# Thirty-two bytes under the feed-forward weights, and later, paced scatters and gathers, in a fused attention and expert kernel

## The chip, the core and the metric

The kernel runs on one core of one Trainium2 chip. The metric is the time of one execution on the device in microseconds (us), the median of several runs. A second, profiled execution left the trace from which all rows below are taken; it has a time of its own.

A core has a matrix engine (TensorE, PE in the rows; its weight loads are PEld), VectorE (DVE), ScalarE (ACT), GpSimd (POOL) and SyncE (SP), each with its own queue of instructions in order. Here SP starts the plain transfers, POOL the indirect ones (gathers and scatters by a table of row numbers), ACT eight loads of weights.

## The reference, cut to what matters

```python
scores = (1 / S) * np.matmul(z, z.transpose(0, 2, 1))        # 8 batches, S = 3072, z is 64 wide
x = u * np.matmul(np.maximum(scores, 0.0) ** 2, v)           # u, v: 8 x 3072 x 256
x = x.reshape(24576, 256)
e = argmax(x @ w_gate); g = softmax weight of e * sigmoid(x @ w_output_gate)[e]
x = g * (np.maximum(x @ w1[e], 0.0) @ w2[e])                 # 8 experts, 256 -> 1024 -> 256
h = x @ w_in; out = (h * sigmoid(h)) @ w_out                 # 256 -> 2048 -> 256
```

Attention without a softmax, then one expert out of eight for each token, then a feed-forward layer for all tokens.

## The kernel before, in words

Every large product is made of three matmuls of rounded 32-bit halves: a value is split into `hi` and `lo` (function `split`, line 104: a copy on ACT or DVE, then a subtraction on DVE), and hi x lo, lo x hi and hi x hi are added up. The matrix engine does them in three stages, one after the other.

**Attention** (line 641). 48 chunks q of 512 rows (six to a batch), each with 24 steps j; 1152 steps k in all. A step is eight matmuls of 512 columns: two for the scores of step k+3 (`s_step`, lines 269 and 270) and six for the values of step k (`v_step`, lines 297 to 299). Between the two stand ACT (`act_r`, line 275; `act_a`, line 280) and DVE (`dve_hl`: `hi` in line 108, `lo` in line 109). The rest is written into tables by step number with `at(k, ...)` and runs behind `dve_hl` of that step: loads of the next batch on SP (`z_load`, `v_load`, `u_load`), splits of its z and v (`z_prep1`, `v_prep`), copies of z's halves over to the other partitions (`z_prep2`, two transfers on SP, lines 198 and 199), and for each finished chunk `x_mul`, `x_hi`, `x_lo`, the transposes `x_tr` into the tile `z` (line 318), and the gate. When a chunk's row numbers are known, 16 scatters on POOL (`x_scatter`, line 466) write its tile `z` into the table `x_d` in device memory. For the first two chunks they are put at step 54 + 16 q + c, for the others spread over 24 steps from step 15 of the next chunk on. `z` has two buffers, so `x_tr` of chunk q waits for the scatters of chunk q-2.

`x_d` has to be zero where no token comes. SP writes the zeros, 26 transfers of up to 1 MB (`zero_pages`, line 165), at steps 5, 9 and 13 and then one in every second step up to 61. The framework orders a scatter and a zero transfer against each other as they stand in the program, since their rows can't be told apart.

`paced(i)` (line 113) lets an indirect transfer wait for the last DVE subtraction in the list `beat`; `dve_hl` and, in the last stage, `h2` append to it. Before the change, the scatters of all chunks but the last, and the gathers of the last stage from block 2 on, are paced.

**Experts** (line 939). 103 pages of 256 tokens, each with one expert, four steps each; 24 matmuls of 256 columns in a step (lines 742 and 763). The weights of a page come by gathers on POOL (line 684), are split on ACT and DVE (`w_split`), and results go out by scatters on POOL (line 770). The scatters of attention that are left over, and the last chunk's (at steps 39 to 54), are issued here. In the last 32 steps the tokens of the feed-forward's block 0 are gathered (line 811) and split.

**Feed-forward** (line 990). 48 blocks m of 512 tokens, 16 steps fc each. A step is twelve matmuls of 512 columns: six for `s2` of step k+3 (line 855) and six for `v2` of step k (lines 877 to 879). Between them ACT takes the sigmoid (line 862) and DVE does three operations (lines 863, 108 and 109, in `h2`). Each block's tokens come by 16 gathers on POOL (`y_gather`, line 811) and are scaled, transposed and split (`y_scale`, `y_tr`, `y_split`). Block 1's 16 gathers stand together between the expert stage and this loop, with no pacing; block 2's are put at fc = 6 to 15 of block 0. The product of line 855 reads `sc` tiles of PSUM of which there are two, so `s2` of step k+3 waits until DVE has read that of step k+1.

**Where tiles lie.** The build gives every tile a byte address in the partition. By their remainder when divided by 128: all operands of attention's large matmuls (`hi`, `lo`, `vh`, `vl`, `hh`, `ll`, `st`) lie at 32; all of the expert stage's (`x1h`, `x1l`, `w0b`, `h1`, `l1`, `w1b`) at 64; in the feed-forward the stationary weights `wi` and `wo` lie at 96, the moving values `yh`, `yl`, `h2`, `l2` at 64, but block 0's `yh0` and `yl0` at 96. The gate's matmuls (line 325) have weights at 32 and moving values at 96. Slices of these tiles begin at multiples of 512 bytes from their start. `wi`, `wo`, `yg0`, `yh0` and `yl0` are in the pool `wr`, which is at the right end of the partition and grows to the left.

Of the kernel before, what the change touches and what calls it, by code (L numbers as in the profile page):

```python
# [8 lines left out]
F32 = mybir.dt.float32  # L9
F32R = mybir.dt.float32r  # L10
# [20 lines left out]
P = 128  # L31
Q = 32
CH = 512
NCH = S // CH
NQ = B * NCH
NJ = S // P
NSTEP = NQ * NJ
NB = CH // Q
# [4 lines left out]
HD = D // 4  # L43
# [5 lines left out]
QL = NQ - 1  # L49
# [3 lines left out]
def fused_kernel(ctx: ExitStack, tc: tile.TileContext, uT, v, zT, wg, w1, w2, w_in, w_out, out):  # L53
# [43 lines left out]
    xp = xs.enter_context(tc.tile_pool(name="xp", bufs=1, side="right", reuse_waits="tile"))  # L97
    att = ExitStack()
    small = att.enter_context(tc.tile_pool(name="small", bufs=1))
    zp = att.enter_context(tc.tile_pool(name="zp", bufs=1))  # L100
# [3 lines left out]
    def split(hi, lo, src, eng="v"):  # L104
        if eng == "a":
            sc.activation(hi, src, AF.Copy)  # L106
        else:
            ve.tensor_copy(hi, src)  # L108
        return ve.tensor_sub(lo, src, hi.bitcast(F32))  # L109

    beat = []

    def paced(i):

        tc.add_manual_dep(
            i.ins, beat[-1].ins.name,
            mybir.DependencyInfo(mybir.DependencyClass.Sync, mybir.DependencyReason.DATA),
            reason="one indirect transfer at a time",
        )
# [64 lines left out]
        ZZ[b, c] = zz  # L184

    def z_prep1(b, c):
        hh = zp.tile([P, CH], F32R, name="hh", tag="hh", bufs=7)
        ll = zp.tile([P, CH], F32R, name="ll", tag="ll", bufs=7)
        split(hh, ll, ZZ.pop((b, c)), "v" if b == 0 and c < 2 else "a")
        HH[b, c], LL[b, c] = hh, ll  # L190

# [110 lines left out]
    XH, XL, Z, G = {}, {}, {}, {}  # L302

    def x_mul(q, dc):
        if dc == 0:
            XH[q] = xp.tile([P, 2, CH], F32R, name="xh", tag="xh", bufs=1)
            XL[q] = xp.tile([P, 2, CH], F32R, name="xl", tag="xl", bufs=1)
            Z[q] = xp.tile([P, NB, HD], F32, name="z", tag="z", bufs=2)
        ve.tensor_mul(UT[q][:, dc, :], ACC[q][dc], UT[q][:, dc, :])

    def x_hi(q, dc):
# [150 lines left out]
    def x_scatter(q, cs=range(NB)):  # L462

        before = XS.setdefault(q, [])
        for c in cs:
            i = gp_.indirect_dma_start(  # L466
                x_u, bass.IndirectOffsetOnAxis(ap=xi4[:, q * NB + c:q * NB + c + 1], axis=0),
                Z[q][:, c, :], None, bounds_check=NSLOT * 4 * T - 1, oob_is_err=False,
            )
            for o in before:  # L470
                tc.declare_no_dep(i.ins, o.ins, reason="scatters to different rows")
            if q < QL:
                paced(i)
            before.append(i)

    def gate_s(q):
# [86 lines left out]
    def at(k, f, *a, pe=False):  # L563
        (pe_tasks if pe else tasks).setdefault(k, []).append((f, a))

    for b in range(1, B):
        first = (b - 1) * NCH * NJ
        last = first + (NCH - 1) * NJ
        for c in range(NCH):
            at(first + c * NJ + 12, z_load, b, c)  # L570
            at(first + c * NJ + 20, z_prep1, b, c)
            at(first + c * NJ + 22 if c < 3 else last + 4 * (c - 3) + 4 if c < NCH - 1 else last + 22,
               z_prep2, b, c)
            s1_ = first + (c + 1) * NJ + 16 if c < 3 else last + (6, 15, 17)[c - 3]
            at(s1_ - 6, v_load, b, c)
            at(s1_, v_prep, b, c, 0)
            at(s1_ + 1, v_prep, b, c, 1)
# [10 lines left out]
    SSTEPS = [15 + (3 * c + 1) // 2 for c in range(NB)]  # L588
    ON_PE = (gate_mm, rank_mm, rep_mm, order1_mm, order2_mm)
    left = []  # L590
    for q in range(NQ - 1):
        for s, f, *a in XTASKS:
            at((q + 1) * NJ + s, f, q, *a, pe=f in ON_PE)
        for c in range(NB):
            k = 54 + q * NB + c if q < 2 else (q + 1) * NJ + SSTEPS[c]
            if k < NSTEP:
                at(k, x_scatter, q, [c])
            else:
                left.append((q, [c]))
# [3 lines left out]
    for job, q in zip(range(2 * NWJ), [q for q in range(1, NQ) if q % NCH < NCH - 1]):  # L603
        k = q * NJ
# [85 lines left out]
    def w_split(k, which):  # L690
        if k >= NS1:
            return
        t, fp = divmod(k, NSUB)
        if which == 0:
            src = raw1[t % 2][:, :, fp * 2 * P:(fp + 1) * 2 * P]
        else:
            src = raw2[t % 2][:, 2 * fp:2 * fp + 2, :]
        w = fp_.tile([P, 2, 2, 2 * P], F32R, name=f"w{which}b", tag=f"w{which}b", bufs=4)
        split(w[:, 0], w[:, 1], src, "a")
        WB[which, k] = w  # L700

    def x_gather(t):
# [30 lines left out]
    def s1(k):  # L733
        t, fp = divmod(k, NSUB)
        ps = ps_s.tile([P, 2, T], F32, name="s1", tag="sc")
        wb = WB.pop((0, k))
        for i in range(2):
            fs = slice(i * P, (i + 1) * P)
            n = 0
            for dc in range(2):  # L740
                for hl, xx in ((1, X1H[t]), (0, X1L[t]), (0, X1H[t])):
                    pe.matmul(ps[:, i, :], wb[:, hl, dc, fs], xx[:, dc, :], start=(n == 0), stop=(n == 5))  # L742
                    n += 1
        hi = mp.tile([P, 2, T], F32R, name="h1", tag="h1", bufs=4)
        lo = mp.tile([P, 2, T], F32R, name="l1", tag="l1", bufs=4)
        sc.activation(hi, ps, AF.Relu)
        ve.scalar_tensor_tensor(lo, ps, 0.0, hi.bitcast(F32), ALU.max, ALU.subtract)  # L747
        H1[k], L1[k] = hi, lo
# [26 lines left out]
    def w_load(dst, o, i):  # L775
        n = 4 * DFF // 4
        sc.dma_start(
            dst.rearrange("p a b c -> p (a b c)")[:, i * n:(i + 1) * n].bitcast(F32),
            wio_d[:, o + i * n:o + (i + 1) * n],
        )  # L780
# [23 lines left out]
    def y_gather(m, cs=range(NB)):  # L804
        if m >= NQ:
            return
        if m > 0 and m not in YG:
            YG[m] = lp.tile([P, NB, HD], F32, name="yg", tag="yg", bufs=3)
        n = (NFIRST if m == 0 else NSLOT) * 4 * T
        for c in cs:  # L810
            i = gp_.indirect_dma_start(  # L811
                YG[m][:, c, :], None, y_u[:n, :],
                bass.IndirectOffsetOnAxis(ap=yi4[:, m * NB + c:m * NB + c + 1], axis=0),
                bounds_check=n - 1, oob_is_err=False,
            )
            if m > 1:
                paced(i)

    def y_scale(m, h):
# [119 lines left out]
    for k in range(NS1):  # L939
        t, fp = divmod(k, NSUB)  # L940
        if k + L1K < NS1:
            s1(k + L1K)
        else:
            s2(k + L1K - NS1)
        for f, a in late.get(k, []):
            if f in ON_PE:
                f(*a)
        v1(k)
        if fp == 0:
            x1_prep(t + 1)  # L950
            if t + 3 >= 4:
                x_gather(t + 3)
        if fp == NSUB - 1 and t < NSLOT - 1:
            y_store(t)
        w_ahead(k)
        if k == NS1 - 24:
            sc.activation(npg, efl, AF.Sigmoid)
        if k in ahead:
            f, *a = ahead[k]
            f(*a)  # L960
        for f, a in late.get(k, []):
            if f not in ON_PE:
                f(*a)
        if k == 120:
            yops = y_index()
        if k > 120 and yops:
            yops.pop(0)()
        if k == 72:
            xs.close()
            wr = moe.enter_context(tc.tile_pool(name="wr", bufs=1, side="right", reuse_waits="tile"))  # L970
            wi = wr.tile([P, 2, 2, DFF], F32R, name="wi")
            wo = wr.tile([P, 2, FC2, D], F32R, name="wo")
            ylast = wr.tile([P, 2, D], F32, name="ylast")
            YG[0] = wr.tile([P, NB, HD], F32, name="yg0")
            YH[0] = wr.tile([P, 2, CH], F32R, name="yh0")
            YL[0] = wr.tile([P, 2, CH], F32R, name="yl0")
        if k in range(80, 160, 10):
            w_load(*((wi, 0), (wo, 4 * DFF))[k >= 120], k // 10 % 4)
    assert not yops
# [3 lines left out]
    for k in range(L1K):  # L983
        h2(k)
    y_store(NSLOT - 1)
    y_gather(1)
    for k in range(L1K, LOOK):
        s2(k)
        h2(k)
    for k in range(NS2):  # L990
        m, fc = divmod(k, FC2)
        if k + LOOK < NS2:
            s2(k + LOOK)
            h2(k + LOOK)
        if fc == 1 and m > 0:
            o_store(m - 1)

        if m > 0:
            y_gather(m + 2, [c for c in range(NB) if fc == 1 + 7 * c // 8])
        elif fc >= 6:  # L1000
            y_gather(2, [c for c in range(NB) if fc == 6 + 9 * c // 15])
        for f, when in ((y_scale, (8, 9) if m == 0 else (3, 4)), (y_tr, (9, 10) if m == 0 else (6, 8)),
                        (y_split, (10, 11) if m == 0 else (7, 9))):
            if fc in when:
                f(m + 1, when.index(fc))
        v2(k)
# [36 lines left out]
```

## Time and profile before

| | |
|---|---|
| Median of the runs | 5558.6 us (5557.41 to 5558.87, 3 runs) |
| Profiled execution: its own time | 5563.38 us |
| its span, first to last instruction | 5561.7 us |
| TensorE busy in the span | 99% |
| DVE, ACT and POOL busy | 80%, 51%, 37% |
| Mean granted clock of TensorE | 0.998 |

The own time of the profiled execution is 1.7 us over its span, and 4.8 us over the median. In the rows, PE's matmuls overlap (the next one starts before the modelled end of the one before), so what a matmul costs is the distance from start to start, not its duration. An idle time in brackets at the end of a row is that before the instruction, with what ended it.

### The profile page before, as it was taken

How to read it: one execution, taken by the hardware profiler on the slowest of the kernel's cores; microseconds unless marked ns; L12 is line 12 of the kernel's file. 1: busy time of each engine (PE TensorE's matmuls, PEld its weight loads, DVE VectorE, ACT ScalarE, POOL GpSimd, SP SyncE). 2: the span in 40 equal slices, each digit the busy share in tenths (PEclk: the TensorE clock that was granted, in tenths of full speed). 3: DMA queues.
4: the chain of work that ended last, by engine and by line, in shares of the span. 5: the costliest groups of instructions: out<-in, count | busy, mean ns of one | idle time of the engine just before them, and what ended most of it. 6: DMA issues, size and time to landing. Idle time of an engine off the chain costs nothing. (4 is left out here: it accounts for less than half of the span.)

```text
span 5561.7 us, 84596 instructions
## 1 busy us (share of the span) xinstructions
PE 5516.5 (99%) x28952; PEld 4694.6 (84%) x28952; DVE 4469.0 (80%) x9832; ACT 2861.0 (51%) x5076; POOL 2055.8 (37%) x1961
## 2 busy tenths in 40 slices
PE   9999999999999999999999999999999999999999
PEld 7788888888888887999999998888888888888887
DVE  8899999999999887878777776777777777777776
ACT  7676777777777766666666664222222222222222
POOL 0433333333333334443333344333333333333331
PEclk9999999999999999999999999999999999999999
DMA  7212121211122101254222221000000000000000
GB/s 259 79 53 60 52 60 53 65 56 56 58 58 58 43 24 54 79 176 140 84 78 76 86 67 35 24 24 24 24 24 24 27 24 24 24 24 24 24 24 20
DMA packets 160243, 314.99 MB, mean 57 GB/s; under 512 B 58560, under 2 KB 66752, under 8 KB 152384
## 3 DMA queue, kind: packets, MB, share of 16 engines
q0 software_dynamic: 95152, 156.97, 9.7%
q1 hardware_dynamic: 63504, 144.22, 8.1%
q10 hardware_dynamic: 1152, 8.39, 0.4%
q8 instruction: 226, 3.70, 0.3%
q14 instruction: 209, 1.71, 0.1%
HBM read 346.83 MB, written 112.72 MB: 83 GB/s over the span
## 5 line engine op out<-in xcount | busy, mean ns | idle before, releaser
L466 POOL DMA_INDIRECT x_d<-z,xi x768 | 794.0, 1034 | 1447.2 <-DVE lo L109 788.5
L811 POOL DMA_INDIRECT yg<-y_d,yi x768 | 807.0, 1051 | 1284.1 <-DVE l L109 1169.5
L862 ACT ACTIVATE sg<-s 128x512 f32<-128x512 f32 x768 | 458.8, 598 | 1599.1 <-PE s L855 1484.0
L855 PE MATMUL s<-yh,wi 128*128 128x512 f32 x3072 | 1089.8, 396 | 5.1 <-DVE sg L863 4.1
L275 ACT ACTIVATE r<-sc 128x512 f32<-128x512 f32 x1152 | 688.8, 598 | 547.3 <-PE sc L270 486.1
L863 DVE TENSOR_TENSOR sg<-s,sg 128x512 f32<-128x512 f32 x768 | 530.7, 691 | 486.6 <-ACT sg L862 480.0
L297 PE MATMUL acc<-hi,vl 128*128 128x512 f32 x2304 | 908.1, 394 | 3.1 <-DVE hi L108 3.1
L298 PE MATMUL acc<-lo,vh 128*128 128x512 f32 x2304 | 900.6, 391 | 1.6 <-DVE lo L109 1.6
L299 PE MATMUL acc<-hi,vh 128*128 128x512 f32 x2304 | 898.3, 390 | 0.0
L109 DVE TENSOR_TENSOR lo<-a,hi 128x512 fp32r<-128x512 f32 x1152 | 798.1, 693 | 39.5
L280 ACT ACTIVATE a<-r 128x512 f32<-128x512 f32 x1152 | 726.2, 630 | 98.8 <-DVE lo L109 73.0
L855 PEld LDWEIGHTS s<-yh,wi 128*128 128x128 f32 x3072 | 577.2, 188 | 145.5 <-DVE sg L863 4.5
L742 PE MATMUL s<-x1h,w0b 128*128 128x256 f32 x3296 | 662.9, 284 | 11.3 <-DVE w0b L109 9.9
L763 PE MATMUL acc<-w1b,h 128*128 128x256 f32 x3296 | 660.7, 283 | 0.0
L877 PE MATMUL acc<-h,wo 128*128 128x512 f32 x1536 | 608.0, 396 | 0.0
L878 PE MATMUL acc<-l,wo 128*128 128x512 f32 x1536 | 608.0, 396 | 0.0
L879 PE MATMUL acc<-h,wo 128*128 128x512 f32 x1536 | 608.0, 396 | 0.0
L855 PE MATMUL s<-yl,wi 128*128 128x512 f32 x1536 | 607.5, 396 | 0.0
L108 DVE CAST hi<-a 128x512 fp32r<-128x512 f32 x1152 | 490.7, 426 | 93.3 <-ACT a L280 83.0
L742 PEld LDWEIGHTS s<-x1h,w0b 128*128 128x128 f32 x3296 | 544.9, 192 | 12.8 <-DVE w0b L109 9.6
L109 DVE TENSOR_TENSOR l<-sg,h 128x512 fp32r<-128x512 f32 x768 | 532.2, 693 | 26.5
L763 PEld LDWEIGHTS acc<-w1b,h 128*128 128x128 f32 x3296 | 543.7, 192 | 0.1
(200 smaller groups left out, 9647.6 us busy)
## 6 DMA issues: line engine op xcount, KB each, us to landing
x_d<-zero SPq DMA_DIRECT2D x25, 1024.0 KB
vr<-in_v_dram SPq DMA_DIRECT2D x48, 512.0 KB
ut<-in_uT_dram SPq DMA_DIRECT2D x48, 512.0 KB
out_dram<-ot SPq DMA_DIRECT2D x48, 512.0 KB
zz<-in_zT_dram SPq DMA_DIRECT2D x96, 128.0 KB
x_d<-z,xi POOLq DMA_INDIRECT x768
yg<-y_d,yi POOLq DMA_INDIRECT x768
st<-hh SPq DMA_DIRECT2D x47, 128.0 KB
```

Source lines behind the costliest of these rows:

```text
L109: return ve.tensor_sub(lo, src, hi.bitcast(F32))
L275: sc.activation(r, SC.pop(k), AF.Relu, scale=1.0 / S)
L280: sc.activation(a, RR.pop(k), AF.Square)
L297: pe.matmul(ACC[q][dc], vl[:, j % 4, ds_], hi, start=(j == 0), stop=False)
L298: pe.matmul(ACC[q][dc], vh[:, j % 4, ds_], lo, start=False, stop=False)
L299: pe.matmul(ACC[q][dc], vh[:, j % 4, ds_], hi, start=False, stop=(j == NJ - 1))
L466: i = gp_.indirect_dma_start(x_u, bass.IndirectOffsetOnAxis(ap=xi4[:, q * NB + c:q * NB + c + 1], axis=0), Z[q][:, c, :], None, bounds_che ...
L742: pe.matmul(ps[:, i, :], wb[:, hl, dc, fs], xx[:, dc, :], start=(n == 0), stop=(n == 5))
L763: pe.matmul(acc[:, h, :], x[:, i, ts], wb[:, hl, i, :], start=first, stop=end, skip_group_check=True)
L811: i = gp_.indirect_dma_start(YG[m][:, c, :], None, y_u[:n, :], bass.IndirectOffsetOnAxis(ap=yi4[:, m * NB + c:m * NB + c + 1], axis=0), bo ...
L855: pe.matmul(ps, wi[:, hl, dc, fs], xx[:, dc, :], start=(n == 0), stop=(n == 5))
L877: pe.matmul(acc, wo[:, 1, fc, es], hi, start=(fc == 0), stop=False)
```

## The change

Five things are done:

- The pool `wr` gets one more tile of 32 bytes at its end. Since the pool's right end stays, `wi`, `wo`, `ylast`, `yg0`, `yh0` and `yl0` begin 32 bytes earlier: at a remainder of 64 by 128 instead of 96. No other tile of the feed-forward moves.
- The scatters of chunk q are issued no earlier than step 76 + 6 (16 q + c) / 5. This moves those of chunks 0 to 7 (chunk 0: steps 54 to 69 before, 76 to 94 after); from chunk 8 on the steps are those of before. `z` gets a third buffer.
- To pay for it, `hh` and `ll` get six buffers in place of seven, and the split of the next batch's z goes from step 20 to 26 after the start of a chunk (step 2 of the chunk that follows), its copies on SP from 22 to 28 where they stood there. Tiles of attention move by 4096 bytes or not at all.
- `w_split` of the expert stage also appends to `beat`, and the last chunk's scatters are paced too. The scatters left over from chunk 46 (ten of them), which waited for a subtraction long done, wait for the newest weight split.
- Block 1's 16 gathers go from the front of the feed-forward loop into block 0's steps fc = 0 to 7, two in a step and paced; block 2's go to fc = 8 to 15, two in a step.

```diff
@@ z_prep1
-        hh = zp.tile([P, CH], F32R, name="hh", tag="hh", bufs=7)
-        ll = zp.tile([P, CH], F32R, name="ll", tag="ll", bufs=7)
+        hh = zp.tile([P, CH], F32R, name="hh", tag="hh", bufs=6)
+        ll = zp.tile([P, CH], F32R, name="ll", tag="ll", bufs=6)
@@ x_mul
-            Z[q] = xp.tile([P, NB, HD], F32, name="z", tag="z", bufs=2)
+            Z[q] = xp.tile([P, NB, HD], F32, name="z", tag="z", bufs=3)
@@ x_scatter
-            if q < QL:
-                paced(i)
+            paced(i)
@@ for b in range(1, B): for c in range(NCH):
-            at(first + c * NJ + 20, z_prep1, b, c)
-            at(first + c * NJ + 22 if c < 3 else last + 4 * (c - 3) + 4 if c < NCH - 1 else last + 22,
+            at(first + c * NJ + 26, z_prep1, b, c)
+            at(first + c * NJ + 28 if c < 3 else last + 4 * (c - 3) + 4 if c < NCH - 1 else last + 28,
                z_prep2, b, c)
@@ for q in range(NQ - 1): for c in range(NB):
-            k = 54 + q * NB + c if q < 2 else (q + 1) * NJ + SSTEPS[c]
+            k = max((q + 1) * NJ + SSTEPS[c], 76 + 6 * (q * NB + c) // 5)
@@ w_split
-        split(w[:, 0], w[:, 1], src, "a")
+        beat.append(split(w[:, 0], w[:, 1], src, "a"))
@@ y_gather
-            if m > 1:
+            if m > 0:
                 paced(i)
@@ pool wr
             YL[0] = wr.tile([P, 2, CH], F32R, name="yl0")
+
+            wr.tile([P, 8], F32, name="wr_gap")
@@ ahead of the feed-forward loop
     y_store(NSLOT - 1)
-    y_gather(1)
@@ in the feed-forward loop
         if m > 0:
             y_gather(m + 2, [c for c in range(NB) if fc == 1 + 7 * c // 8])
-        elif fc >= 6:
-            y_gather(2, [c for c in range(NB) if fc == 6 + 9 * c // 15])
+        elif fc < 8:
+            y_gather(1, [2 * fc, 2 * fc + 1])
+        else:
+            y_gather(2, [2 * fc - 16, 2 * fc - 15])
```

## Rows read from the trace of the kernel before

**Rows 1.** The page's first part: busy time, share and instructions of each engine.

```profile
PE 5516.5 (99%) x28952; PEld 4694.6 (84%) x28952; DVE 4469.0 (80%) x9832; ACT 2861.0 (51%) x5076; POOL 2055.8 (37%) x1961
```

**Rows 2.** Windows: length, busy us (count) of PE, PEld, DVE, ACT, POOL; PEclk; DMA.

```profile
104.00:150.00 46.00, 45.61 (x208) 36.89 (x207) 40.55 (x119) 30.86 (x55) 9.09 (x8) 1.00 0.53 183
150.00:210.00 60.00, 49.51 (x206) 39.17 (x205) 44.46 (x128) 31.95 (x58) 30.02 (x30) 0.89 0.22 67
210.00:255.00 45.00, 45.00 (x207) 36.88 (x206) 41.47 (x121) 31.11 (x55) 16.22 (x17) 1.00 0.14 42
500.00:2100.00 1600.00, 1598.74 (x7279) 1307.11 (x7279) 1464.85 (x4231) 1123.26 (x1966) 584.77 (x569) 1.00 0.18 53
...
2400.00:3300.00 900.00, 899.86 (x7499) 899.62 (x7497) 688.21 (x1114) 589.99 (x1094) 340.04 (x312) 1.00 0.32 105
3405.00:3440.00 35.00, 29.90 (x121) 23.49 (x120) 20.15 (x34) 5.82 (x11) 22.07 (x22) 0.95 0.11 24
...
3500.00:5500.00 2000.00, 2000.00 (x8573) 1610.11 (x8572) 1457.34 (x2414) 518.25 (x894) 738.07 (x704) 1.00 0.09 24
```

**Rows 3.** Timeline of PE, attention: start us, duration us, instruction.

```profile
561.92 0.39 PE L269 MATMUL sc<-hh,st 128*128 128x512 f32 x1
...
570.99 0.39 PE L269 MATMUL sc<-hh,st 128*128 128x512 f32 x1
```

**Rows 4.** Timeline of PE, two score products of the feed-forward's block 0.

```profile
3402.00 0.39 PE L855 MATMUL s<-yh,wi 128*128 128x512 f32 x1
...
3404.73 0.40 PE L877 MATMUL acc<-h,wo 128*128 128x512 f32 x1
```

**Rows 5.** Waits between 140 and 195 us: who for whom, us, times, longest.

```profile
ACT r L275 <- remote: 8.7, 1, 8.7
...
PE sc L269 <- ACT r L275: 7.6, 2, 7.2
POOL x_d L466 <- DMA x_d<-zero: 7.3, 1, 7.3
...
DVE z L318 <- DMA x_d<-z,xi: 6.2, 1, 6.2
```

**Rows 6.** Waits of SP's queue over the whole span.

```profile
SPq L165 <- DMA x_d<-z,xi: 37.0, 4, 13.4
```

**Rows 7.** Timeline of POOL, first scatter, and a run of scatters.

```profile
116.36 1.17 POOL L466 DMA_INDIRECT x_d<-z,xi  x1 [113.20 <-DVE lo L109]
...
154.01 1.40 POOL L466 DMA_INDIRECT x_d<-z,xi  x1 [5.54 <-DVE hi L108]
...
182.32 0.97 POOL L466 DMA_INDIRECT x_d<-z,xi  x1 [0.30 <-issue]
```

**Rows 8.** Timeline of ACT at the start of the feed-forward.

```profile
3425.45 0.60 ACT L862 ACTIVATE sg<-s 128x512 f32<-128x512 f32 x1 [5.11 <-PE s L855]
3432.57 1.09 ACT L862 ACTIVATE sg<-s 128x512 f32<-128x512 f32 x2 [6.52 <-remote]
```

**Rows 9.** Timeline of POOL there: the ends of two runs of gathers.

```profile
3406.65 1.05 POOL L811 DMA_INDIRECT yg<-y_d,yi  x1 [2.53 <-DVE l L109]
...
3429.65 0.99 POOL L811 DMA_INDIRECT yg<-y_d,yi  x1 [0.30 <-issue]
3435.42 1.00 POOL L811 DMA_INDIRECT yg<-y_d,yi  x1 [4.78 <-DVE l L109]
...
3453.99 1.00 POOL L811 DMA_INDIRECT yg<-y_d,yi  x1 [0.51 <-issue]
```

**Rows 10.** Timeline of DVE at the change from attention to experts.

```profile
2199.56 0.71 DVE L724 STREAM_TRANSPOSE xt<-xg 128x512 f32<-128x512 f32 x1 [9.35 <-DMA xg<-x_d,xidx]
```

**Rows 11.** The tile `ll`: its instruction, count, ns min/median/max, first and last start.

```profile
L109 DVE TENSOR_TENSOR ll<-zz,hh x48: 682/686/727, 5.9 to 1919.4; 128x512 fp32r<-128x512 f32 x48
```

**Rows 12.** Line 325, the gate's matmuls: the same columns.

```profile
L325 PE MATMUL lg<-xl,gm x96: 394/396/403, 68.4 to 2253.4; 128*128 128x512 f32 x96
```

**Rows 13.** Timeline of DVE in a batch's last chunk, around step 8.

```profile
539.11 0.69 DVE L109 TENSOR_TENSOR vl<-vr,vh 128x512 fp32r<-128x512 f32 x1 [1.48 <-ACT vh L106]
```

## The prediction, made before the changed kernel was run

> **What bounds the kernel now.** I read the busy shares first. TensorE is busy 99% of the span, the next engine 80% [rows 1], so the time is what its matmuls cost from start to start, plus its few gaps. The windows of the three stages come next [rows 2]. They give three costs. In attention, 40 matmuls of 512 columns lie between the two rows of [rows 3]: 570.99 - 561.92 = 9.07 us, 226.75 ns each. In the expert stage 7499 matmuls of 256 columns fill 900 us: 120.0 ns each. In the feed-forward 8573 matmuls of 512 columns fill 2000 us: 233.3 ns each. At the granted clock of 1.00 (the level of 2.4 GHz) 512 columns are 213.3 ns and 256 are 106.7 ns. So attention and experts both pay 13.3 ns on each matmul, and the feed-forward pays 20.0 ns on each. The reader is to see that the same kind of matmul is 6.6 ns dearer in the last stage, with no engine behind: DVE is busy 73% there, POOL 37%.
>
> The windows also show where TensorE stood still. From 104 to 150 us it did 208 matmuls and from 150 to 210 us 206; from 3405 to 3440 us it did 121. The waits and the queues then say why [rows 5 to 9].
>
> **The change, part by part.**
>
> *The 32 bytes.* In attention and in the expert stage stationary and moving tiles have the same remainder by 128; in the feed-forward they are 32 apart. The trace holds one trial of this: block 0's `yh0` and `yl0` lie as `wi` does. Two score products of that block that run without other matmuls between them, twelve matmuls of line 855, take 3404.73 - 3402.00 = 2.73 us [rows 4], 227.5 ns each, with the same `wi` that costs 233.3 ns from block 1 on. After the change all operands of the stage lie at 64, as in the expert stage. Bounds: nothing, if the position is not the cause; 6.67 ns each (233.33 - 226.67), if it is. I take the upper one, since the same line of code shows it. The stage has 48 x 16 x 12 = 9216 matmuls: 9216 x 6.67 ns = 61.4 us, less 0.2 us for block 0, whose score products have a part of it already: 61.2 us. DVE covers this: 1457.3 us of work in 2000 us would stand in 1943 us, 75%. Without that cover a step would cost what DVE needs, and that is below 2.1 us against 2.72 us of TensorE.
>
> The Trainium skill speaks against this part. "TensorE: Matmul & The Clock Gate", Part 2 (step 1), says that TensorE has two independent SBUF read ports, one for the moving operand and one for weight loads, so that loading the next weights takes nothing from the running matmul; by that, 32 bytes change nothing and this term is 0. The 227.5 ns and 233.3 ns of one line do not agree with it.
>
> *The first scatters.* Zero transfers stand at steps up to 61, the first scatters at 54 to 69. The two are ordered by the program, so that they wait for one another: four zero transfers waited 37.0 us for scatters [rows 6], and scatters for zeros [rows 5]. The first scatter ran at 116.36 us, and those held up then came as a run: from 154.01 to 182.32 us, 21 of them [rows 7]. What SP has queued behind the zeros (z, v, u) came late, `x_tr` waited 6.2 us for a buffer of `z`, and ACT stood still for 8.7 us with no releaser that the profile names, while POOL ran through its backlog [rows 5]. TensorE paid. Attention does 7279 matmuls in 1600 us, 4.55 per us; with 2 more that overlap a window's ends, 46 us should hold 211.3 and 60 us 275. Missing are 3.3 and 69, and 72.3 x 0.2198 us = 15.9 us. That holds the time at the lower granted clock too (0.89 on average from 150 to 210 us). After the change the last zero is put at step 61 and the first scatter at step 76, 28 us later at 1.875 us a step (45 us by 24); no zero waits for a scatter. The scatters then come every 1.2 steps (2.2 us, against 1.0 to 1.4 us of POOL each). The last of chunk 0 is at step 94, and chunk 3's `x_tr`, which now needs that buffer, at step 100: 11 us later. What is late next would be that transpose. Bounds: nothing (another wait takes it up) to 15.9 us; I take 15.9, as from 210 us on, with scatters spread, 45 us hold 207 [rows 2].
>
> *The splits of z.* 42 splits of 0.69 us on DVE [rows 11], and as many copies on ACT, go from step 20 to step 2 of the next chunk, where DVE has more to do. Bounds: nothing, to all of them exposed, 42 x 0.686 = 28.8 us. I take nothing. Over 1600 us of attention TensorE's busy time lacks 1.3 us [rows 2], and in the heaviest chunk, a batch's last, DVE itself waits 1.48 us for ACT around step 8 [rows 13]; a delay of 0.69 us at step 2 disappears in that. The copies behind them on SP are due 13 steps later at the earliest (24 us).
>
> *Pacing in the expert stage.* Waits are put in POOL's queue, and queued behind them are weight gathers, page gathers and result scatters. A paced scatter waits for a weight split of its own step. Where that step also issues a weight gather, this gather waits for the same split already. Bounds: nothing to one step of 2.88 us for each of the 26 scatters, 75 us, if POOL were the bound; it is busy 340 of 900 us there [rows 2], and pages are gathered three ahead. I take nothing.
>
> *The start of the feed-forward.* Block 1's 16 gathers and the first two of block 2 ran without a pause, 18 from 3406.65 to 3429.65 us, 1.35 us each [rows 9]. ACT's sigmoids came later and later, at 3425.45 and 3432.57 us, the last after 6.52 us with no releaser named [rows 8], and recovered 1.9 us behind the run's last gather. TensorE did 121 matmuls in 35 us where 4.29 per us and 2 at the ends make 152: 31 x 0.233 = 7.2 us, the lower clock behind the gap in it (0.95 on average). After the change the 32 gathers come two in a step of 2.72 us, 1.36 us each: the same rate, but POOL waits for DVE in each step, so that an ACT that falls behind stops the gathers. The nearest row is the paced run, 13 from 3435.42 to 3453.99 us, 1.55 us each, in which TensorE lost nothing. Bounds: 0 to 7.2 us; I take 7.2. Block 1's last gather is then put at step 7 and the scaling that needs it at step 9, 5.4 us later, against 2.7 us for two gathers and their landing: little room, and what is late next.
>
> *The change from attention to experts.* DVE waits 9.35 us for the first page [rows 10], whose gather stands in POOL's queue behind the same scatters as before. Nothing is changed there: 0.
>
> **The sum.** 61.2 + 15.9 + 7.2 = 84.3 us. From the profiled execution's own 5563.4 us that leaves 5479.1 us. That execution is 4.8 us above the median of the runs, so for a median I say 5558.6 - 84.3 = 5474.3, rounded to 5474 us.
>
> **The rivals.**
>
> - *The gathers still hold ACT up.* Their rate is that of the run that did it. Against it stands that POOL now waits on what ACT feeds. All 7.2 us kept: 5481.5 us.
> - *The early stall comes back in another place*, as a wait of `x_tr` for scatters that start 22 steps later, or of a load behind the zeros. For it: DMA is busy 53% from 104 to 150 us; against it, the 11 us of room. Half to all of 15.9 us kept: 5482 to 5490 us.
> - *DVE pays for the moved splits.* Half exposed 5489 us, all of it 5503 us. Against it: the 1.48 us of idle time.
> - *The position of the weights does not matter*, the port rule worked as a mechanism: 233.3 ns stay, 5474.3 + 61.2 = 5535.5 us. Against it: [rows 4].
> - *Slower.* What counts is not lying alike, and 64 and 64 collide more than 96 and 64. The gate's matmuls, 64 apart, last 396 ns [rows 12], as long as in the feed-forward, so that the pattern is not one I know. If the step goes as far up as it should go down, 240 ns, the time is 5474.3 + 122.6 = 5597 us. It decides from 2.5 ns a matmul (23.1 us / 9216), a distance of 235.8 ns. Against it: the expert stage lies at 64 and 64 and pays the same 13.3 ns as attention.
>
> **How the numbers follow.** The forecast, 5466 to 5480 us, has 0.62; gathers 0.15; early stall 0.09; DVE 0.04; port rule 0.05; slower 0.02; a gain beyond the sum, in a gap I count as unchanged, 0.03. From 5465 to 5492 us lie the first three and half of DVE's, some 0.85. About 0.2% (11 us) is what a measurement can tell from no change. Faster 0.97, same 0.01, slower 0.02.
>
> **What would show it.** Feed-forward: 2000 us hold 8823 matmuls (226.7 ns) and line 855's mean falls towards attention's. Up to 210 us, no zero transfer waits for a scatter, the first scatter runs near 155 us, and the 45 us windows hold 207 each. From 3380 us on (the stage starts some 16 us earlier), no sigmoid waits 5 us. The 9 us wait ahead of the experts stays. I am wrong if the matmuls stay at 233 ns, or if DVE's moved splits open gaps at a chunk's first steps.

## Result, and the profile after

| | before | changed |
|---|---|---|
| Median of the runs | 5558.7 us (5557.4 to 5561.8, 4 runs) | 5480.7 us (5476.8 to 5483.7, 4 runs) |
| Profiled execution: its own time | 5563.38 us | 5476.75 us |
| its span | 5561.7 us | 5475.0 us |

The ratio is 0.9857, with a 95% interval from 0.9845 to 0.9869: 78 us less by the medians, 86.6 us less by the profiled executions. Forecast were 5474 us and a sum of 84.3 us. The median lies 0.7 us above the range of 5466 to 5480 us that had a chance of 0.62, and inside 5465 to 5492 us, which had 0.85. In the changed kernel, lines behind `w_split` and `y_gather` stand one lower (855 is 854, 862 is 861, 877 to 879 are 876 to 878, 724 is 723).

First the busy shares of the changed kernel. Against [rows 1] DVE, ACT and POOL have nearly the work they had; PE is busy 67 us less with as many matmuls, so most of the gain is in what a matmul costs, not in gaps.

```profile
PE 5449.3 (100%) x28952; PEld 4690.0 (86%) x28952; DVE 4481.3 (82%) x9832; ACT 2866.0 (52%) x5076; POOL 2071.7 (38%) x1961
```

Then its windows (length, busy us and count of PE, PEld, DVE, ACT, POOL; PEclk; DMA).

```profile
104.00:150.00 46.00, 46.00 (x211) 37.72 (x210) 43.04 (x126) 32.67 (x58) 0.00 (x0) 1.00 0.59 204
150.00:210.00 60.00, 60.00 (x273) 49.22 (x272) 56.60 (x156) 42.79 (x77) 25.09 (x24) 1.00 0.22 64
500.00:2100.00 1600.00, 1598.81 (x7272) 1307.23 (x7271) 1467.95 (x4194) 1123.21 (x1968) 594.52 (x569) 1.00 0.19 53
2400.00:3300.00 900.00, 899.87 (x7498) 899.62 (x7498) 688.47 (x1114) 589.77 (x1093) 343.07 (x314) 1.00 0.32 105
3390.00:3425.00 35.00, 34.39 (x151) 27.81 (x150) 25.79 (x43) 8.38 (x15) 25.17 (x24) 1.00 0.12 23
3500.00:5400.00 1900.00, 1900.00 (x8384) 1573.28 (x8383) 1426.96 (x2356) 510.91 (x873) 729.41 (x695) 1.00 0.09 25
```

In the feed-forward 1900 / 8384 = 226.6 ns a matmul, where [rows 2] gave 233.3. Attention and experts are as they were. From 104 to 210 us stand 484 matmuls instead of 414, and the granted clock is 1.00 all through. In 35 us at the start of the feed-forward there are 151 instead of 121.

POOL's timeline shows the scatters' new start: the first at 157.60 us instead of 116.36 [rows 7], behind no zero transfer but with pauses that DVE ends.

```profile
157.60 1.18 POOL L466 DMA_INDIRECT x_d<-z,xi  x1 [154.43 <-DVE lo L109]
159.24 0.99 POOL L466 DMA_INDIRECT x_d<-z,xi  x1 [0.46 <-DVE lo L109]
```

The waits of SP's queue no longer hold the 37.0 us of [rows 6] (line 165 for scatters), and between 140 and 195 us nobody waits 8.7 us for `remote` [rows 5].

ACT's sigmoids at the start of the feed-forward, the same view as [rows 8]:

```profile
3400.04 0.60 ACT L861 ACTIVATE sg<-s 128x512 f32<-128x512 f32 x1 [3.26 <-PE s L854]
3404.40 0.60 ACT L861 ACTIVATE sg<-s 128x512 f32<-128x512 f32 x1 [3.76 <-PE s L854]
3405.95 0.60 ACT L861 ACTIVATE sg<-s 128x512 f32<-128x512 f32 x1 [0.95 <-PE acc L878]
3407.47 0.60 ACT L861 ACTIVATE sg<-s 128x512 f32<-128x512 f32 x1 [0.93 <-PE s L854]
```

A step is 2.72 us, a sigmoid 0.60, so an idle time of 2.12 is even running. Here two come late (3.26, 3.76) and the next two catch up. The lateness is there, but in this execution it stays under 3 us, and PE loses 1.15 us in all (0.28, 0.11, 0.65 and 0.11 by its starts) where it lost 7.2.

At the change from attention to experts DVE still waits for the first page, 9.11 us where [rows 10] had 9.35:

```profile
2182.12 0.71 DVE L723 STREAM_TRANSPOSE xt<-xg 128x512 f32<-128x512 f32 x1 [9.11 <-DMA xg<-x_d,xidx]
```

Put side by side by the starts of PE's instructions, the profiled executions differ by 1.0 us before the first scatter, 16.1 us more by step 96, 0.2 us at the wait for the first page, 2.2 us in the expert stage and 67.0 us from its end on.

### The profile page after: what moved, and what is told of

It reads as the page before. It is cut to its first block, busy times and chain, and to the rows that moved or that the text cites. A ratio compares the mean times of both kernels' runs of the same rounds, so it can differ in the third digit from the quotient of the medians.

```text
span 5475.0 us, 84633 instructions
## 1 busy us (share of the span) xinstructions
PE 5449.3 (100%) x28952; PEld 4690.0 (86%) x28952; DVE 4481.3 (82%) x9832; ACT 2866.0 (52%) x5076; POOL 2071.7 (38%) x1961
## 4 chain that ended last, share of the span: by engine, by line
PE 96%; DVE 2%; issue 1%; DMA 0%; ACT 0%; POOL 0%; POOLq 0%; SPq 0%; DVEq 0%; ACTq 0%
PE s L854 19%; PE s L741 11%; PE acc L762 11%; PE acc L297 9%; PE acc L298 9%; PE acc L299 9%; PE acc L878 6%; PE acc L877 6%; PE acc L876 6%; PE sc L269 4%; PE sc L270 4%; PE lg L325 1%; DVE lo L109 0%; DVE hi L108 0%; DVE vl L109 0%
## 5 line engine op out<-in xcount | busy, mean ns | idle before, releaser
L854 PE MATMUL s<-yh,wi 128*128 128x512 f32 x3072 | 1070.4, 389 | 0.1
L878 PE MATMUL acc<-h,wo 128*128 128x512 f32 x1536 | 597.5, 389 | 0.0
L876 PE MATMUL acc<-h,wo 128*128 128x512 f32 x1536 | 597.5, 389 | 0.0
```

The lines of the kernel that those rows point to most:

```text
L854: pe.matmul(ps, wi[:, hl, dc, fs], xx[:, dc, :], start=(n == 0), stop=(n == 5))
L876: pe.matmul(acc, wo[:, 1, fc, es], hi, start=(fc == 0), stop=False)
L878: pe.matmul(acc, wo[:, 0, fc, es], hi, start=False, stop=(fc == FC2 - 1))
```

## Experiments

They ran on two chips. On the first (e1_gap_only to e4_gap96) the kernel before took 5545.0 us, on the other 5562.2 and 5560.4 us; each ratio is to the kernel before on the same chip.

### What the 32 bytes do

Of a matmul's two operands, the stationary one is loaded as weights and the moving one is streamed against it.

The tile alone, in the kernel before (e1_gap_only):

```diff
             YL[0] = wr.tile([P, 2, CH], F32R, name="yl0")
+            wr.tile([P, 8], F32, name="wr_gap")
```

> The kernel before with the 32-byte tile alone. Theory (position of the weights): 9216 matmuls of the feed-forward go from 233.3 to 226.7 ns, the time falls by 61 us to about 5497 us, and the two stalls (15.9 us early, 7.2 us at the start of the feed-forward) stay. Rival (weight loads and moving values do not touch each other, and the gain came from a stage that is entered without a stall): the matmuls stay at 233.3 ns and the time at 5558 us.

Measured: 5483.3 us, ratio 0.9888 (0.9871 to 0.9904), 61.8 us less. Its window in the feed-forward:

```profile
3500.00:5400.00 1900.00, 1900.00 (x8384) 1574.57 (x8383) 1426.97 (x2357) 511.06 (x874) 731.01 (x697) 1.00 0.09 25
```

All the rest without it (e2_no_gap; the same line, taken out of the changed kernel):

> The changed kernel without the 32-byte tile. Theory: matmuls of the feed-forward at 233.3 ns, both stalls gone, 5558.7 - 23 = 5536 us. Rival (the parts do not add up: a slower feed-forward gives ACT more room and hides what is left of its hold-up): under 5534 us.

Measured: 5538.2 us, ratio 0.9987 (0.9978 to 0.9997), 6.9 us less. The time is close to the expected 5536 us, but the gain is not the expected one: 23 us less were meant, and the kernel before is itself faster on this chip (the last section comes back to it).

```profile
3500.00:5400.00 1900.00, 1900.00 (x8145) 1529.58 (x8144) 1384.23 (x2291) 491.03 (x847) 712.83 (x680) 1.00 0.09 24
```

1900 / 8145 = 233.3 ns with all other edits in place, 226.6 ns with the tile alone. The two kernels tell which edit does it; three more tell what about it does. They are the changed kernel with another length of the tile:

```diff
-            wr.tile([P, 8], F32, name="wr_gap")
+            wr.tile([P, 16], F32, name="wr_gap")    # e3_gap64; 24 in e4_gap96, 40 in e5_gap160
```

> The changed kernel with 64 bytes in place of 32, so that the weights lie at remainder 32 by 128 and the moving values at 64: 32 apart, the other way. Theory (lying alike is what counts): 233.3 ns as before the change, 5481 + 61 = 5542 us. Rival (the weights' own position counts, 96 is a bad place, whatever the moving values do): 226.7 ns and 5481 us.

> The changed kernel with 96 bytes: weights at 0, moving values at 64, 64 apart, as in the gate's matmuls. If what counts is the remainder by 64: 226.7 ns and 5481 us. If it is the remainder by 128 or more: between 230 and 240 ns, 5512 to 5604 us.

> The changed kernel with a gap of 160 bytes in place of 32: the weights lie at a remainder of 64 by 128, as the moving values do, but 128 bytes off by 512. If the remainder by 128 is what counts, feed-forward matmuls stay at 226.7 ns and the time is that of the changed kernel (0 to 3 us apart). If the remainder by a longer stretch (256 or 512 bytes) counts, they cost 229 to 233 ns and the time is 20 to 60 us longer.

The windows of the three, e3_gap64, e4_gap96 and e5_gap160:

```profile
3500.00:5400.00 1900.00, 1900.00 (x8145) 1529.20 (x8144) 1382.92 (x2290) 491.76 (x848) 713.05 (x680) 1.00 0.09 24
```

```profile
3500.00:5400.00 1900.00, 1900.00 (x8303) 1559.03 (x8302) 1411.98 (x2336) 503.85 (x865) 726.56 (x693) 1.00 0.09 25
```

```profile
3500.00:5400.00 1900.00, 1900.00 (x8178) 1540.21 (x8177) 1390.23 (x2301) 494.00 (x851) 715.53 (x683) 1.00 0.09 24
```

| kernel | weights, by 512 | moving, by 512 | apart | ns from start to start | time, us |
|---|---|---|---|---|---|
| before, e2_no_gap | 480 | 448 | 32 | 233.3 | 5538.2 (e2) |
| changed, e1_gap_only | 448 | 448 | 0 | 226.6 | 5483.3 (e1) |
| e3_gap64 | 416 | 448 | 32 | 233.3 | 5537.7 (one run) |
| e4_gap96 | 384 | 448 | 64 | 228.8 | 5497.9 (one run) |
| e5_gap160 | 320 | 448 | 128 | 232.3 | 5534.6 (two runs, second chip) |

Which of the two lies lower does not matter (e3_gap64). 64 bytes apart costs a third of what 32 do; neither of the two costs expected for e4_gap96 (226.7 ns, or 230 to 240) came true. And e5_gap160, which lies alike by 128, pays nearly in full: the remainder by 128 is not the measure. A multiple of 512 apart is alike (the weights' slices step by 512 bytes); whether 256 would do was not run. In e4_gap96 the cost is not even: from line 876's start to 877's it is 232 ns, from there to 878's 226, from there to the next 876's 229. The groups by line show the same alternation in the durations (their columns: busy us, mean ns).

```profile
L876 PE MATMUL acc<-h,wo 128*128 128x512 f32 x1536 | 605.2, 394 | 0.0
L878 PE MATMUL acc<-h,wo 128*128 128x512 f32 x1536 | 602.1, 392 | 0.0
L877 PE MATMUL acc<-l,wo 128*128 128x512 f32 x1536 | 596.1, 388 | 0.0
```

In the changed kernel the same three lines are 389 ns each.

### The early scatters

The scatters' and z's edits, without the others, in the kernel before (e6_scatters_only):

```diff
+            k = max((q + 1) * NJ + SSTEPS[c], 76 + 6 * (q * NB + c) // 5)
...
+            Z[q] = xp.tile([P, NB, HD], F32, name="z", tag="z", bufs=3)
...
+            at(first + c * NJ + 26, z_prep1, b, c)      # hh, ll: 6 buffers; z_prep2 28
```

> The kernel before with the later scatters, the third buffer of z and the moved splits alone. Theory: the time falls by what the kernel before loses between 104 and 210 us on the same chip (5 to 16 us), and nothing else moves. Rival (the moved splits cost DVE time): less than that, with gaps of TensorE in the first steps of chunks.

Measured: 5545.0 us, ratio 0.9970 (0.9958 to 0.9981), 17.2 us less. Its windows early on are those of the changed kernel:

```profile
104.00:150.00 46.00, 46.00 (x211) 37.71 (x210) 43.01 (x126) 32.38 (x58) 0.00 (x0) 1.00 0.58 202
150.00:210.00 60.00, 60.00 (x273) 49.23 (x272) 56.61 (x157) 42.74 (x77) 25.08 (x24) 1.00 0.21 62
```

The stall at the start of the feed-forward is still there in that kernel (3.55 us in one gap of PE). By the starts of PE's instructions its trace is ahead of the kernel before on that chip (e0_before_again, below) by 0.6 us at the first scatter, by 14.8 us at 210 us, and by 2.2 us more behind the start of the feed-forward, where it has no edit. So some 14 of the 17.2 us are the early stall, and the rest differs from execution to execution.

The splits of z alone (e9_z_moved_only):

```diff
-            at(first + c * NJ + 20, z_prep1, b, c)
+            at(first + c * NJ + 26, z_prep1, b, c)      # and z_prep2 from 22 to 28
```

> The kernel before with nothing but the next batch's z split at step 26 in place of 20 and copied from step 28 in place of 22. Prediction's step: hidden, so within 2 us of the kernel before, early stall and all. Rival: the 42 subtractions of 0.69 us on DVE are exposed in part, 5 to 29 us slower, with a gap of PE at steps 2 and 3 of a chunk. A third way: the moved copies on SP stand behind the zeros no longer, and part of the early stall of some 16 us goes with that alone.

Measured: 5562.3 us, ratio 1.0002 (0.9993 to 1.0011). The windows of 150 to 210 us and of attention as a whole:

```profile
150.00:210.00 60.00, 48.23 (x202) 38.28 (x201) 42.07 (x121) 30.48 (x56) 29.59 (x29) 0.91 0.22 66
500.00:2100.00 1600.00, 1598.76 (x7280) 1307.14 (x7279) 1469.84 (x4233) 1122.03 (x1966) 593.49 (x569) 1.00 0.18 53
```

The early stall is there as in [rows 2], and PE's busy time over 1600 us is that of before (1598.74). So the moved splits neither cost nor bring anything, and the early gain of e6_scatters_only belongs to the later scatters (with the third buffer of `z`, which was not run alone).

### The start of the feed-forward

The kernel before once more, for the size of the stall on that chip (e0_before_again):

> The kernel before once more, for a trace from the chip of this call, since the stalls may differ from chip to chip. Theory (both stalls follow from the order of the instructions): 16 us lost from 104 to 210 us and 7 us at the start of the feed-forward, as in the first trace. Rival (only the waits that the program orders, zeros against scatters, are the same everywhere; the time without a named releaser is the chip's): 3 to 6 us early, nothing in the feed-forward, 5541 to 5549 us.

Measured: 5561.7 us. Sigmoids came 4.31, 7.97 and 3.93 us behind their products. Its window:

```profile
3405.00:3440.00 35.00, 30.10 (x117) 23.54 (x116) 18.92 (x32) 6.34 (x11) 22.00 (x22) 0.90 0.10 20
```

The gathers' edits alone (e7_gathers_only: block 1's gathers moved into steps 0 to 7 and paced, block 2's into 8 to 15):

```diff
-            if m > 1:
+            if m > 0:
                 paced(i)
...
-    y_gather(1)
...
-        elif fc >= 6:
-            y_gather(2, [c for c in range(NB) if fc == 6 + 9 * c // 15])
+        elif fc < 8:
+            y_gather(1, [2 * fc, 2 * fc + 1])
+        else:
+            y_gather(2, [2 * fc - 16, 2 * fc - 15])
```

> The kernel before with the gathers of blocks 1 and 2 moved and paced alone. Theory: the time falls by what the kernel before loses at the start of the feed-forward on the same chip: 7 us where ACT is held up, nothing where it is not. Rival (the new place costs something itself, since block 1's last gather comes just ahead of its use): 1 to 3 us slower where there was nothing to gain.

Measured: 5554.2 us, ratio 0.9987 (0.9978 to 0.9997), 8.0 us less.

```profile
3410.00:3445.00 35.00, 34.57 (x149) 27.59 (x149) 24.33 (x41) 9.00 (x15) 23.97 (x24) 1.00 0.11 22
```

At 4.29 per us and 2 at the ends 35 us hold 152; here are 149 with the clock at 1.00. Late sigmoids remain, by up to 3.26 us.

The changed kernel with block 1's gathers in their new place, but not paced (e8_unpaced):

```diff
-            if m > 0:
+            if m > 1:
                 paced(i)
```

> The changed kernel with block 1's gathers at their new place, but without the wait on DVE. Theory (the wait is what stops POOL when ACT is behind): where the chip holds ACT up, a stall of 3 to 7 us comes back; where it does not, no difference. Rival (the place alone, two in a step, is enough, since POOL gets the next pair only when its queue comes to it): no difference anywhere.

Measured: 5482.8 us (2 runs), ratio 0.9858 (0.9838 to 0.9877); its time cannot be told from the changed kernel's, the trace can. POOL, PE and ACT in that run, three timelines of one stretch:

```profile
3405.21 1.00 POOL L810 DMA_INDIRECT yg<-y_d,yi  x1 [0.30 <-issue]
3406.51 1.00 POOL L810 DMA_INDIRECT yg<-y_d,yi  x1 [0.30 <-issue]
3407.82 1.00 POOL L810 DMA_INDIRECT yg<-y_d,yi  x1 [0.31 <-issue]
3409.12 1.05 POOL L810 DMA_INDIRECT yg<-y_d,yi  x1 [0.30 <-issue]
3416.49 1.20 POOL L810 DMA_INDIRECT yg<-y_d,yi  x1 [6.32 <-DVE l L109]
```

```profile
3405.77 0.39 PE L854 MATMUL s<-yh,wi 128*128 128x512 f32 x1
...
3407.16 0.39 PE L878 MATMUL acc<-h,wo 128*128 128x512 f32 x1
3408.83 0.50 PE L854 MATMUL s<-yh,wi 128*128 128x512 f32 x1 [1.28 <-issue]
```

```profile
3407.45 0.60 ACT L861 ACTIVATE sg<-s 128x512 f32<-128x512 f32 x1 [3.72 <-PE s L854]
3411.78 1.08 ACT L861 ACTIVATE sg<-s 128x512 f32<-128x512 f32 x2 [3.73 <-PE s L854]
```

The product that the last sigmoid waits for ended at 3405.77 + 0.39 = 3406.16 us. ACT did nothing, and started 5.6 us later. POOL stood at its gathers without a pause until 3410.17 us. PE lost 3.4 us here in three gaps (1.44, 1.48 and 0.51), against 1.15 in the changed kernel. But the changed kernel once more on this chip (e10_after_again, below) had sigmoids up to 3.8 us late. The windows of e8_unpaced and of e10_after_again:

```profile
3390.00:3425.00 35.00, 32.40 (x141) 25.84 (x139) 23.03 (x39) 7.82 (x14) 22.03 (x21) 1.00 0.10 20
```

```profile
3390.00:3425.00 35.00, 33.76 (x147) 26.75 (x145) 23.86 (x40) 7.84 (x13) 24.23 (x24) 1.00 0.11 23
```

At 226.6 ns 35 us hold 156 matmuls: 15 are missing without pacing (3.4 us), 9 and 5 with it (2.0 us here, 1.1 in the changed kernel's first trace). So pacing is worth one or two of the 7 us, by three single executions, and the new place of the gathers the rest.

### The wait ahead of the experts

The changed kernel again on the second chip (e10_after_again), beside one in which the scatters of chunk 46 that stand in attention's last nine steps are issued behind the change of stage, with those already left over (b1_left):

```diff
-            if k < NSTEP:
+            if k < NSTEP - 9:
                 at(k, x_scatter, q, [c])
```

> The changed kernel again, beside the others on the same chip: 5475 to 5485 us, a ratio of 0.985 to 0.990 to the kernel before.

> The changed kernel, with those of chunk 46's last scatters that stand in attention's last nine steps moved behind the change of stage, so that the first pages' gathers stand earlier in POOL's queue. If POOL's queue holds the first page up, the wait ahead of the experts (9.1 us in the changed kernel) shrinks and the time falls by up to 9 us. Rival: the first gathers wait for attention's own last rows anyway; wait and time stay (within 2 us).

Measured: e10_after_again 5478.5 us (5476.1 to 5482.9, 4 runs), ratio 0.9856 (0.9840 to 0.9871). b1_left 5473.3 us (5470.8 to 5475.3, 5 runs), ratio 0.9843 (0.9830 to 0.9857). The runs of the two do not overlap, their intervals do. DVE's row for the first page, and PE's waits from 2160 to 2260 us, in b1_left:

```profile
2174.69 0.71 DVE L723 STREAM_TRANSPOSE xt<-xg 128x512 f32<-128x512 f32 x1 [1.57 <-DMA xg<-x_d,xidx]
```

```profile
PE s L741 <- DVE w0b L109: 2.1, 2, 1.4
PE s L741 <- issue: 1.1, 1, 1.1
```

The same waits of the changed kernel, and then the windows from 2150 to 2200 us, of the changed kernel and of b1_left:

```profile
PE s L741 <- DVE w0b L109: 9.7, 2, 8.9
```

```profile
2150.00:2200.00 50.00, 40.33 (x223) 35.01 (x222) 31.93 (x89) 25.29 (x44) 21.97 (x22) 0.90 0.31 114
```

```profile
2150.00:2200.00 50.00, 47.25 (x294) 41.72 (x293) 38.52 (x99) 30.85 (x54) 21.67 (x20) 1.00 0.34 117
```

POOL's timeline of the changed kernel (the last of six scatters that b1_left has behind the change of stage, and the first page's gather), and then the same gather in b1_left:

```profile
2174.57 0.97 POOL L466 DMA_INDIRECT x_d<-z,xi  x1 [0.30 <-issue]
...
2177.48 1.01 POOL L705 DMA_INDIRECT xg<-x_d,xidx  x1 [0.59 <-issue]
```

```profile
2170.89 1.28 POOL L705 DMA_INDIRECT xg<-x_d,xidx  x1 [6.67 <-PE sc L270]
```

The first page waited for its place in POOL's queue, behind six scatters. By its starts PE's first gap there is 1.6 us instead of 9.1, and the clock stays at its upper level (2.4 GHz), where the changed kernel spends part of that stretch at 1.2 GHz behind the gap (0.90 on average). Some of the gain goes to smaller waits behind it. This is the fastest kernel that was run.

## Why the prediction held, step by step

- **The 32 bytes: right, by the mechanism and by the size.** 61.2 us were forecast; the edit alone gave 61.8, and 9216 x (233.3 - 226.6) is 62. [Rows 4], two products of a block whose tiles happened to lie as the weights do, had shown it without any change. The rule of the Trainium skill that was weighed against it ("TensorE: Matmul & The Clock Gate", Part 2, step 1: two independent read ports, so that loading weights takes nothing from the running matmul) does not agree with these runs: where the weights lie, and nothing else, makes the same matmul cost 226.6 or 233.3 ns.
- **What "alike" means was wrong in the working.** The prediction and the description before it go by the remainder by 128. e5_gap160 is alike by 128 and pays 232.3 ns. That the sum held all the same was luck: all big tiles of attention and experts are alike by 512 as well, and so are the feed-forward's after the change. It also answers what the rival of a slow 64-and-64 was built on: the gate's matmuls [rows 12] are 64 apart by 128, but 192 apart by 512, and are no trial of a distance of 64; e4_gap96 is, and costs 228.8 ns. From start to start the gate's own take 234 to 236 ns (medians, kernel before).
- **The first scatters: the size right, the reason in part.** 15.9 us forecast; 16.1 us between the profiled executions, 14.2 in the trace of e6_scatters_only. Nothing came late next: the third buffer's transpose never waits for a scatter. But PE's longest gap (7.2 us) stands behind ACT's 8.7 us with no releaser [rows 5], and what ACT waited for are the late signals of the last section. On the first chip, where no signal was late, the same order of zeros and scatters (SP's zeros waited 35.9 us) cost 29 matmuls, 6.4 us. By that comparison some 6 of the 15.9 us are what the order of the instructions costs by itself; the rest the prediction had as ACT's idle time, without its cause.
- **The splits of z: right at nothing** (e9_z_moved_only, within 0.1%). The bound of 28.8 us had no part in it.
- **Pacing in the expert stage: nothing, as forecast.** From 2400 to 3300 us there are 7498 matmuls, 7499 before. This edit was not run alone.
- **The start of the feed-forward: the size right, the reason half right.** 7.2 us forecast, 8.0 by e7_gathers_only, some 6 of 7.2 in the changed kernel's trace. But the rival's mechanism (gathers hold ACT up) is still at work: sigmoids are late by up to 2.8 us, in e10_after_again by up to 3.8. PE stands still only as far as the lateness passes what two `sc` tiles, into which line 855 writes, can bridge (1.1 and 2.0 us in the two traces). Pacing and spreading keep it near that; they do not remove it.
- **The sum.** From the profiled execution it was 84.3 us against 86.6 measured. The surplus is 1.0 us at the start and 2.2 us of small waits at the end of the expert stage, which no edit can be named for: they add up to 1.3 us there in the changed kernel, to 3.6 or more in e4_gap96 and b1_left, which share its edits, and to 3.4 in the kernel before. By the medians the gain is 78 us, with e10_after_again on the second chip 81.8 us; the profiled execution of before lay above its median and that of the changed kernel below its own, which accounts for 8.6 us between the two ways of counting. The predicted 5474 us is thus 6.7 us below the median: taking a sum from one execution to a median of others carries that much.

## What to carry to other kernels

Where an engine is busy 99% of the time, compare the start-to-start cost of like instructions between stages: a few ns that recur 9216 times were worth more here than all visible gaps together, and the cause stood in the tiles' addresses (keep stationary and moving operands a multiple of 512 bytes apart in the partition, and look again after any change of tile sizes). Long unbroken runs of indirect transfers on POOL are to be spread over steps at the changes of stage, even where POOL itself is no bound; on one of the two chips such a run cost 7 to 8 us here, on the other nothing. An edit that moves a wait is priced by the wait that ends last there: the 9 us ahead of the experts lay in plain view before, and six scatters moved behind it won 5 us (medians of four and five runs).

## What the runs showed of the hardware that was not expected

- **TensorE's signals arrive late while POOL works through a long run of gathers.** In e8_unpaced the trace's semaphore events show it: matmuls that count up PE's semaphore ended at 3400.56, 3401.92, 3403.28, 3404.64 and 3406.17 us, and the counts stand at 3403.11, 3404.59, 3407.43, 3409.62 and 3411.76 us, 2.6 to 5.6 us behind; the last of these is the first of four between 3411.76 and 3411.99 us, 1.6 us behind the end of the run's last gather. ACT's sigmoids start 0.02 us behind the first, third and fifth of them. So neither ACT nor PE was slow, as the prediction had it of ACT. The kernel before has the same early on: its scatters pause at 184.94 us, the counts of matmuls that had ended by 180.09 us come in a bunch from 186.62 to 186.84 us, and ACT starts at 186.65 us. In both traces some events of such stretches are missing. Why the counts wait is open.
- **It differed between the two chips.** On the first chip e1_gap_only ran 18 gathers without a pause from 3394.24 us on, 1.30 to 1.48 us apart, and the counts came 0.01 us behind the matmuls. Its window there has every matmul; the early one, put ahead of it, lacks 29 of 275:

```profile
150.00:210.00 60.00, 57.19 (x246) 46.06 (x245) 52.13 (x142) 38.70 (x69) 35.60 (x34) 0.94 0.23 69
...
3393.00:3428.00 35.00, 35.00 (x156) 29.01 (x155) 27.27 (x46) 8.69 (x16) 26.15 (x26) 1.00 0.11 23
```

  The 32 bytes are not the reason: e8_unpaced has them too. On the first chip the edits other than the 32 bytes brought 6.9 us (e2_no_gap), on the second 17.2 and 8.0 in two kernels that sum to 25.2.
- **The position costs in steps.** 0, 64, 128 and 32 bytes apart cost 226.6, 228.8, 232.3 and 233.3 ns a matmul of 512 columns with a weight load of its own. The cost hangs on where the two operands lie against each other, not on where either lies (e3_gap64 and the kernel before); by what means is not shown. And it is not a matter of one matmul's two operands alone: in e4_gap96 the score products of block 0, 0 apart but run between value products that are 64 apart, cost 231.3 ns each, where those of the later blocks cost 228.9; in the kernel before they cost 230.1 ns on average, and 227.5 where twelve run together [rows 4]. The Trainium skill, "SBUF — State Buffer" (SBUF: two separate sides), says that PE never waits on anyone there. Between engines nothing here speaks against that; for TensorE's own two operands these numbers show a cost that it does not name.
